# Attention, routed experts and soft experts on one core: a written order of finer steps on every engine up to the experts, and gates made per pair of batches

## The chip, the core and the metric

The kernel runs on one core of a Trainium2 chip. The core has five engines that work side by side, each through its own list of instructions in order: PE (TensorE, matmuls into the accumulation memory PSUM), DVE (VectorE), ACT (ScalarE), POOL (GpSimd) and SP (SyncE, which here only starts DMA transfers). POOL also starts the transfers that gather or scatter rows by an index. An instruction that waits for a semaphore holds up all that stands behind it on its engine. The metric is the device time of one execution in microseconds (us); lower is better.

## The reference

```python
# attention: 8 batches, 8 heads, 576 positions, head size 64
q_s = softmax(q over head dim);  k_s = softmax(k over positions)
kv  = einsum('bhsd,bhse->bhde', k_s, v)
x   = einsum('bhsd,bhde->bhse', q_s, kv)          # laid out as 4608 tokens x 512
# routed experts: 8 experts, 512 -> 1024 -> 512, the best two of each token
logits = x @ w_gate
noisy  = logits + log1p(exp(x @ w_noise)) * noise
top2, top2_w = the two largest of noisy, softmax over the two
out[mask] += top2_w * (relu(x[mask] @ w1[e]) @ w2[e])    # for each expert e
# soft experts on out: 32 slots, softmax over tokens in, softmax over slots out
```

## The kernel before

The 8 batches are worked on as four pairs, numbered 0 to 3; a pair has nine tiles of 128 tokens (TP = 9), 36 tiles in all. The text string FIRST lists the work up to the experts as short steps, and MIX lists the rest of pair 3, which is spread over the first expert blocks, a few steps after each part of a block.

For one pair i the steps are: load k, v and q (`lk`, `lv`, `lq`); the maximum of k over positions, by a DVE maximum over tiles and then PE transposes (`km`); subtract it (`ks`) and take the exponential on ACT (`ke`); the q maximum on DVE (`qm`), its subtraction on POOL (`qs`, L255) and exponential on ACT (`qe`); the product of k and v on PE (`kv`, L277 and L278, four column groups c for each of the two batches b), whose DVE scaling into the tile KB starts with L282; KB transposed and multiplied by the gate weights (`kt`, `kw`); for each of nine tiles j the q transpose on PE (`qt`, L265) and the output product (`ou`, L308), scaled out of PSUM either by DVE (L327, L328) or, with an `a` behind the step, by eight ACT instructions (L324). The scaled tile goes to the table xtab in DRAM. Then `he` adds the eight heads' logits, and `ga` starts a gate: it makes noisy logits, picks the best two experts and counts places. A gate is a generator; each `bg` lets the oldest one go on to its next yield. Before, a pair has two gates, one of six tiles and one of three (GT = 6). Inside a gate, L436 and L437 build a one-hot matrix of rows (`ob`), L445 one of columns (`oa`), and L455 multiplies them on PE.

After the gates of pairs 0 and 1 (18 tiles) `pf` (plan_first) plans the first ten expert blocks: POOL copies eight stretches of a table into the index tile pl_ia (L614), and two gathers (L709) fetch the token rows pl_x of the first block. SP can load that block's weights once pl_eba is known. A block needs its weights split into a high and a low part (L763: R1h on ACT, R1l on DVE, and so on for R2, R0) and its rows transposed on PE (L781) and split (xh on ACT, xl on DVE, L783); then the first expert product runs (L796). MIX runs beside the first nine blocks; the other blocks follow, and a last stage does the soft experts.

What sets the order: FIRST and MIX give only the order in which the program text issues steps. The framework's scheduler then orders each engine's list itself, by its own estimates of durations, so that an instruction can stand well ahead of or behind its place in FIRST.

Of the kernel before, what the change touches and what calls it, by code (L numbers as in the profile page):

```python
# [21 lines left out]
P = 128  # L22
# [14 lines left out]
GT = 6  # L37
# [9 lines left out]
lk0 se lv0 lq0.0 lq0.1 lq0.2 lk1 lq1.0 lq1.1 lq1.2 km0.0 ks0.0 km0.1 qm0.0 qs0.0 qe0.0 qm0.1 qs0.1m qm0.2 ke0.0 ks0.1v ke0.1 qm1.0 km1.0 qs1.0 bg bg kv0.0 kv0.0 kv0.1 kt0.0 qe0.1 qs0.2 ks1.0 kv0.1 kt0.1 qt0.0 qe0.2 kw0.0 lv1 qm1.1 qt0.1 bg km1.1 qt0.2 bg ks1.1 ou0.0 qm1.2 ke1.1 bg bg bg ou0.1 qt0.3 qs1.2 qs1.1 lk2 qt0.4 bg qt0.5 bg ou0.2 kw0.1 ou0.3 bg ke1.0 qt0.6 ou0.4 qt0.7 bg qt0.8 ou0.5a bg qe1.1 he0.1 lq2.0 bg he0.0v qe1.2 lq2.1 ou0.6 lq2.2 ou0.7a qe1.0 bg ou0.8a he0.2 bg bg bg bg bg km2.0 bg bg kv1.0 ga0.0 kv1.0 ga0.1 kt1.0 kv1.1 qt1.0 qt1.1 kw1.0 qm2.0 bg qm2.1 ks2.0 kv1.1 bg ou1.0 km2.1 lv2 kt1.1 qt1.2 ks2.1 bg qm2.2 lq3.0 ou1.1 qs2.0 bg lk3 qt1.3 qs2.2 bg qt1.4 ke2.1 qs2.1 qt1.5 bg kw1.1 ou1.2 bg ou1.3 ou1.4 ze qt1.6 qe2.1 qt1.7 ke2.0 bg he1.0v ou1.5a qt1.8 bg bg bg bg lq3.1 lq3.2 ou1.6a ou1.7 he1.1v ze bg qe2.0 bg ou1.8 bg he1.2 qe2.2 kv2.0 bg ga1.0 ga1.1 pf km3.0 bg bg kv2.0 kt2.0 qm3.0 ks3.0 bg bg qt2.0 kv2.1 kv2.1 km3.1 bg kw2.0 kt2.1 qm3.1 qt2.1 ze lv3 bg qt2.2 ks3.1 qm3.2 qs3.2 ou2.0 qt2.3 ou2.1 qs3.0 ze qs3.1 bg qt2.4 bg bg ou2.2a ke3.1 bg ou2.3 qt2.5 kw2.1 ou2.4a ou2.5a qt2.6 bg bg qt2.7 qt2.8 ou2.6a he2.0 bg bg bg he2.1 qe3.1 ke3.0 ou2.7 bg ou2.8a he2.2 bg bg bg bg bg kv3.0 kv3.0 kv3.1 kt3.0 qe3.2 kw3.0 kv3.1 qe3.0 kt3.1 kw3.1  # L47
# [3 lines left out]
ga2.0 ga2.1 qt3.0 bg bg bg bg bg ou3.0a qt3.1 bg bg bg qt3.2 bg ou3.1a bg qt3.3 ou3.2 bg qt3.4 bg he3.0 ou3.3 bg qt3.5 bg ou3.4 bg bg bg bg ze ze qt3.6 bg ze bg ou3.5a bg bg qt3.7 bg bg ze he3.1 ou3.6a bg ou3.7 qt3.8 ou3.8 bg bg bg bg bg bg bg he3.2 bg bg bg ga3.0 bg ga3.1 bg bg bg bg pl bg bg bg bg bg bg bg bg bg bg bg bg bg bg bg  # L51
# [60 lines left out]
def attention(k):  # L112
# [3 lines left out]
    with ExitStack() as ctx:  # L116
# [72 lines left out]
        def setup():  # L189
# [10 lines left out]
            nc.vector.memset(cnt, 0.0)  # L200
            nc.vector.memset(tab, 0.0)


        def k_max(i, b):
            kt = kts[i]
            m2 = e2.tile([P, 2, D], F32, name="m2")
# [1165 lines left out]
```

## Time and profile before

| | before |
|---|---|
| median of 3 runs | 1235.06 us (1233.3 to 1235.41) |
| profiled execution: its time / the span of its instructions | 1234.64 us / 1232.9 us |
| busy share of the span | PE 93%, DVE 65%, ACT 47%, POOL 27% |
| first expert product (L796) starts | 193.83 us after the span's start |
| PE busy before it / in the rest of the span | 146.89 us of 193.8 / 1001.29 us of 1039.1 |

A timeline row gives start, duration, engine, line, operation, output tile <- input tiles, shape and the number of instructions merged; in brackets stands the idle time of that engine just before, and who ended it. A window row gives for a stretch the busy time of each engine (with its instructions), then the clock granted to PE (1.00 is 2.4 GHz, 0.50 is 1.2 GHz), the mean busy share of the DMA engines and GB/s. PE works on nearly without a break from the first expert product on; ahead of it, it does not.

### The profile page before, as it was taken

To read this page: it belongs to the slowest core of one execution; us is meant where nothing else is said; L and a number is where in the kernel's file an instruction comes from. 1 tells how busy PE (TensorE), PEld (TensorE's weight loads), DVE (VectorE), ACT (ScalarE), POOL (GpSimd) and SP (SyncE) were. 2 spreads that over 40 slices of the span, in tenths; PEclk is the share of its full clock that TensorE was granted. 3 is DMA by queue.
4 is the path that set the end of the run, shared out by engine and by line. 5 is a ranking of instruction groups with operands and counts; after the bars stand their busy time and mean duration, and the time that the engine had idled before them with its cause. 6 is when DMAs were issued, how large, how long until landed. Compare 5 with 4: busy or idle time off the path is not lost. (4 is left out here: it accounts for less than half of the span.)

```text
span 1232.9 us, 21326 instructions
## 1 busy us (share of the span) xinstructions
PE 1148.2 (93%) x7808; PEld 997.7 (81%) x7808; DVE 802.4 (65%) x1493; ACT 580.7 (47%) x879; POOL 326.9 (27%) x376
## 2 busy tenths in 40 slices
PE   6776989999999999999999999999999999969994
PEld 5665878998888998889978998998998998956542
DVE  7889777678876665555556666666666666646653
ACT  3554666464444444434434454544444454424324
POOL 3353251343242322112222322322321321310000
PEclk9788899999999999999999999999999999988997
DMA  9847471796446475556668564563846353237797
GB/s 342 289 143 274 155 263 40 198 290 186 113 106 180 111 215 148 144 163 169 170 176 264 139 199 104 148 193 85 220 108 171 47 151 78 45 69 287 260 356 307
DMA packets 116107, 219.10 MB, mean 178 GB/s; under 512 B 13968, under 2 KB 54032, under 8 KB 111888
## 3 DMA queue, kind: packets, MB, share of 16 engines
q1 hardware_dynamic: 98944, 177.11, 41.8%
q0 software_dynamic: 17040, 40.44, 17.2%
q8 instruction: 67, 1.10, 0.4%
q14 instruction: 56, 0.46, 0.1%
HBM read 243.31 MB, written 49.70 MB: 238 GB/s over the span
## 5 line engine op out<-in xcount | busy, mean ns | idle before, releaser
L763 DVE TENSOR_TENSOR R1l<-ringS,R1h 128x1024 fp32r<-128x1024 f32 x96 | 117.8, 1227 | 102.7 <-ACT R1h L763 100.2
L763 DVE TENSOR_TENSOR R0l<-ringS,R0h 128x1024 fp32r<-128x1024 f32 x95 | 116.4, 1225 | 104.1 <-ACT R0h L763 103.5
L763 ACT ACTIVATE R1h<-ringS 128x1024 fp32r<-128x1024 f32 x96 | 101.7, 1060 | 141.0 <-PE py L826 85.0
L763 ACT ACTIVATE R0h<-ringS 128x1024 fp32r<-128x1024 f32 x95 | 100.8, 1061 | 138.4 <-PE py L826 75.3
L763 DVE TENSOR_TENSOR R2l<-ringS,R2h 128x1024 fp32r<-128x1024 f32 x91 | 111.4, 1225 | 81.2 <-ACT R2h L763 78.7
L763 ACT ACTIVATE R2h<-ringS 128x1024 fp32r<-128x1024 f32 x91 | 96.5, 1060 | 136.2 <-PE py L826 72.6
L796 PE MATMUL ph<-xh,R0h 128*128 128x256 f32 x400 | 113.3, 283 | 2.5 <-ACT R2h L763 2.4
L796 PE MATMUL ph<-xl,R0h 128*128 128x256 f32 x400 | 113.4, 283 | 0.0
L796 PE MATMUL ph<-xh,R0l 128*128 128x256 f32 x400 | 112.9, 282 | 0.0
L800 DVE SCALAR_TENSOR_TENSOR hl<-ph,hh 128x512 fp32r<-128x512 f32 x140 | 95.7, 684 | 24.0 <-ACT hh L799 24.0
L709 POOL DMA_INDIRECT xg<-xtab,pl_idx x40 | 49.2, 1229 | 216.7 <-DVE sc L786 198.1
L796 PE MATMUL ph<-xh,R2h 128*128 128x256 f32 x360 | 102.2, 284 | 1.9 <-DVE hl L800 1.9
L796 PE MATMUL ph<-xl,R2h 128*128 128x256 f32 x360 | 102.0, 283 | 0.5 <-DVE xl L783 0.5
L796 PE MATMUL ph<-xh,R2l 128*128 128x256 f32 x360 | 101.8, 283 | 0.0
L796 PE MATMUL ph<-xh,R1h 128*128 128x256 f32 x360 | 100.7, 280 | 0.2 <-DVE hl L800 0.2
L796 PE MATMUL ph<-xl,R1h 128*128 128x256 f32 x360 | 100.3, 279 | 0.0
L796 PE MATMUL ph<-xh,R1l 128*128 128x256 f32 x360 | 100.3, 279 | 0.0
L832 POOL DMA_INDIRECT x<-y,pl_idx x40 | 63.5, 1588 | 129.0 <-DVE y L831 118.9
L799 ACT ACTIVATE hh<-ph 128x512 fp32r<-128x512 f32 x140 | 81.6, 583 | 32.5 <-PE ph L796 32.5
L826 PE MATMUL py<-R1l,hh 128*128 128x512 f32 x200 | 79.7, 399 | 0.0
L796 PEld LDWEIGHTS ph<-xh,R0h 128*128 128x128 f32 x400 | 76.2, 191 | 3.8 <-ACT R2h L763 2.8
L826 PE MATMUL py<-R1h,hl 128*128 128x512 f32 x200 | 78.8, 395 | 0.0
(439 smaller groups left out, 3064.6 us busy)
## 6 DMA issues: line engine op xcount, KB each, us to landing
ringS<-in_moe_w_dram SPq DMA_DIRECT2D x292, 512.0 KB
ringA<-in_moe_w_dram SPq DMA_DIRECT2D x12, 1024.0 KB
ringA<-in_moe_w_dram SPq DMA_DIRECT2D x22, 512.0 KB
xtab<-xr SPq DMA_DIRECT2D x36, 256.0 KB
kt<-in_k_dram SPq DMA_DIRECT2D x8, 1024.0 KB
v<-in_v_dram SPq DMA_DIRECT2D x8, 1024.0 KB
x<-z SPq DMA_DIRECT2D x5, 1280.0 KB
ringS<-x SPq DMA_DIRECT2D x5, 1024.0 KB
```

The costliest lines, as they stand in the source:

```text
L709: k.nc.gpsimd.indirect_dma_start(out=x, out_offset=None, in_=k.xtab[:n], in_offset=bass.IndirectOffsetOnAxis(ap=idx, axis=0))
L763: turn[1:] = [nc.scalar.activation(r[0], f, AF.Copy), nc.vector.tensor_sub(r[1], f, r[0].bitcast(F32))]
L796: nc.tensor.matmul(ph[:, g, :], w[i][:, c, g * P:(g + 1) * P], x[:, c, :], start=n == 0, stop=n == 11)
L799: nc.scalar.activation(hh[:, fs, :], ph, AF.Relu)
L800: nc.vector.scalar_tensor_tensor(hl[:, fs, :], ph, 0.0, hh[:, fs, :].bitcast(F32), op0=ALU.max, op1=ALU.subtract)
L826: nc.tensor.matmul(py[s], a[h], w[i][:, f, :], start=u == 4 and f == n == 0, stop=u == 7 and f == 1 and n == 2)
L832: d = nc.gpsimd.indirect_dma_start(out=k.x2[:NTOK // 2] if b < NPA else k.x2, out_offset=bass.IndirectOffsetOnAxis(ap=at(b, s), axis=0), i ...
```

## The change

There are four parts.

1. All of FIRST now stands under `tc.manual_schedule` for PE, DVE, ACT, POOL and SP: each engine takes its instructions in the order in which FIRST issues them, and the scheduler only places later work among them. FIRST is rewritten: 439 steps in place of 243.
2. The steps are finer. What one step issued on two or three engines is now one step per engine: k maximum, its transposes, its reduction (`km`, `kn`, `ko`, `kp`), one subtraction and one exponential per part of k (`ks`, `ke` with a third number), q transpose and its copy (`qt`, `qu`), KB scaling, transposes and copies (`kb`, `kt`, `ku`, `kw`, `kx`), and output product, sums, scaling, logits and store (`ou`, then `os oa ol st` or `ov st`). MIX is rewritten too: 135 steps in place of 85.
3. A pair has one gate of nine tiles (GN allots room for 18; each `ga` asks for 9), with a yield between any two engines' turns. The sum of the heads' logits goes to a tile of its own (`ls`). The product of `ge` with the triangle moves from POOL to DVE and both are float16. `ob` is built per three tiles in two buffers.
4. In FIRST, 13 of 27 tiles are scaled by ACT (10 before), the q subtraction of three of twelve groups is on DVE (`qs2.0v`, `qs3.1v`, `qs3.2v`; before, two thirds of one), the head sums of two groups are on DVE (three before). v of pair 0 is loaded after q of pair 0 and k of pair 1 (before: right after k of pair 0). The gate of pair 2 starts in FIRST's last part but is carried on in MIX.

```diff
-GT = 6
+GN, GT = 2 * TP, TP
-lk0 se lv0 lq0.0 lq0.1 lq0.2 lk1 lq1.0 lq1.1 lq1.2 km0.0 ks0.0 km0.1 qm0.0 qs0.0 qe0.0 ...
+lk0 lq0.0 lq0.2 se lq0.1 lk1 lv0 lq1.2 lq1.1 lq1.0 lv1 kf0 km0.0 kg0 kn0.0 qm0.0 km0.1 qs0.0 ...
...
+        def km_tr(i, b):
+            pk = psk["km", i, b] = k.pt([P, 4, P])
...
+        def k_sub(i, b, x):
+            ms = psk["ms", i, b].rearrange("p c d -> p (c d)")
+            kp = k_part(i, b, x)
+            nc.vector.tensor_sub(kp, kp, ms[b * 64:b * 64 + 64] if x == 2 else bcast(ms, 1, 2))
...
         def q_tr(i, j):
-            pq = k.pt([P, 4, P])
+            pq = psk["q", i, j] = k.pt([P, 4, P])
...
+        def q_copy(i, j):
             qTs[i, j] = ap.tile([P, 4, P], F32, name="qT", bufs=4)
-            nc.scalar.copy(qTs[i, j], pq)
+            nc.scalar.copy(qTs[i, j], psk.pop(("q", i, j)))
...
+            eng.tensor_add(lss[i // 2][:, j:j + T1 - T0], lr[:, :, 0], lr[:, :, 1])
-        def gate(T0, T1):
-            n_t = T1 - T0
+        def gate(i, n):
+            T0, n_t = i * TP, n * TP
+            T1 = T0 + n_t
...
-            ge = full("ge", [P, GT, E, E])
+            ge = full("ge", [P, GN, E, E], F16)
+            yield
             nc.vector.tensor_tensor(ge, bcast(n, 2, E), bcast(n, 3, E), op=ALU.is_ge)
-            yield 1
-            nc.gpsimd.tensor_tensor(ge, ge, bcast(k.tril, 1, n_t), op=ALU.mult)
+            nc.vector.tensor_tensor(ge, ge, bcast(k.tril, 1, n_t), op=ALU.mult)
...
+            for h in range(0, n_t, GT):
+                pa = pr.tile([P, E, T1], F32, name="pk")
+                for m0 in range(0, GT, CW // 2):
+                    ms, ml = slice(h + m0, h + m0 + CW // 2), slice(m0, m0 + CW // 2)
+                    ob = sp.tile([P, CW // 2, P, 2], F16, name="ob", bufs=2)
...
-        for st in FIRST.split():
-            step(st)
-        back(99)
+        with tc.manual_schedule(engines={e.engine for e in (nc.tensor, nc.vector, nc.scalar, nc.gpsimd, nc.sync)}):
+            for st in FIRST.split():
+                step(st)
+            back(99)
```

How the lists move, at three places. First PE at the program's start, before (pv is the k-v product, pt a transpose, km the k maximum, mT its reduced form):

```order
L215 MATMUL pt<-ident,kt 128x128 x4
L219 MATMUL pt<-ident,km 128x128 x4
L229 MATMUL pt<-ident,mT 128x128 x4
L219 MATMUL pt<-ident,km 128x128 x4
L277 MATMUL pv<-v_159,kt 128x129 x4
L229 MATMUL pt<-ident,mT 128x128 x4
L278 MATMUL pv<-v_159,kt 128x129
```

and now:

```order
L223 MATMUL pt<-ident,kt 128x128 x4
L240 MATMUL pt<-ident,km 128x128 x8
L251 MATMUL pt<-ident,mT 128x128 x4
L285 MATMUL pt<-ident,q_143 128x128 x12
L251 MATMUL pt<-ident,mT 128x128 x4
L223 MATMUL pt<-ident,kt 128x128 x4
L285 MATMUL pt<-ident,q_143 128x128 x4
L240 MATMUL pt<-ident,km 128x128 x4
L298 MATMUL pv<-v_171,kt 128x129 x4
L299 MATMUL pv<-v_171,kt 128x129
```

The k-v product of pair 0 has moved behind four q transposes and the first transposes of pair 1. Next DVE where the first gate meets the k-v product of pair 1, before (rk is the first DVE instruction behind a k-v product; c, s, dl, rw, ln belong to gates):

```order
L354 TENSOR_SCALAR w<-u 128x24
L400 TENSOR_REDUCE c_815<-s_805 128x8
L360 SCALAR_TENSOR_TENSOR dl<-w,u 128x24
L362 RECIPROCAL rw<-w 128x24
L405 TENSOR_REDUCE s<-n 128x6
L282 TENSOR_SCALAR rk<-pv 128x4
L406 TENSOR_SCALAR s<-s 128x6
L283 RECIPROCAL rk<-rk 128x4
L407 RECIPROCAL s<-s 128x6
L286 TENSOR_TENSOR KB_129<-pv,rk 64x4x64 x2
```

and now:

```order
L402 SCALAR_TENSOR_TENSOR g_701<-ls 128x72
L275 TENSOR_TENSOR q_531<-q_531,qm 128x1536
L307 TENSOR_SCALAR rk<-pv 128x4
L308 RECIPROCAL rk<-rk 128x4
L311 TENSOR_TENSOR KB_131<-pv,rk 64x4x64 x2
L408 TENSOR_SCALAR g_706<-g_703 128x72
L307 TENSOR_SCALAR rk<-pv 128x4
L308 RECIPROCAL rk<-rk 128x4
L311 TENSOR_TENSOR KB_132<-pv,rk 64x4x64 x2
L259 TENSOR_TENSOR kt<-kt,pt 128x1024
L415 SCALAR_TENSOR_TENSOR g_755<-g_706,g_703 128x72
L417 RECIPROCAL g_759<-g_706 128x72
```

The gate's instructions (now 72 columns) stand between whole pieces of pair work, and at this point the gate has only begun. Last, DVE where the first expert block begins, before (R1l, R2l are weight halves, xl the low part of the rows, ob and oa the one-hot matrices of pair 2's gate):

```order
L445 TENSOR_TENSOR oa<-cols,af 128x3x384 x2
L745 MEMSET gn 128x3
L436 TENSOR_TENSOR ob<-cols,bf 128x768 x2
L400 TENSOR_REDUCE c_3466<-s_3459 128x8
L405 TENSOR_REDUCE s<-n 128x3
L763 TENSOR_TENSOR R1l<-ringS,R1h 128x1024
L437 TENSOR_TENSOR ob<-ob,tok_112 128x768
L763 TENSOR_TENSOR R2l<-ringS,R2h 128x1024
L437 TENSOR_TENSOR ob<-ob,tok_112 128x768
L406 TENSOR_SCALAR s<-s 128x3
L763 TENSOR_TENSOR R0l<-ringS,R0h 128x1024
L783 TENSOR_TENSOR xl<-ph_1845,xh 128x4x128
```

and now:

```order
L653 TENSOR_TENSOR pl_done<-pl_done,pl_tf 128x8
L268 TENSOR_REDUCE qm<-qt 128x24
L697 SCALAR_TENSOR_TENSOR pl_at<-pl_done,pl_so 128x8
L774 MEMSET gn 128x3
L275 TENSOR_TENSOR qt<-qt,qm 128x1536
L268 TENSOR_REDUCE qm<-qt 128x24
L812 TENSOR_TENSOR xl<-ph_1747,xh 128x4x128
L815 SCALAR_TENSOR_TENSOR sc,gn<-pl_x_1671,pl_eoa 128x8
L422 SCALAR_TENSOR_TENSOR ln<-ls,ln 128x72
L792 TENSOR_TENSOR R1l<-ringS,R1h 128x1024
L812 TENSOR_TENSOR xl<-ph_1756,xh 128x4x128
```

Pair 2's one-hot matrices are gone from this place, xl stands ahead of the weight halves, and maxima and subtractions of pair 3's q stand in their place.

## Rows read from the trace of the kernel before

**Rows 1.** The page: busy time of each engine, share of the span.

```profile
PE 1148.2 (93%) x7808; PEld 997.7 (81%) x7808; DVE 802.4 (65%) x1493; ACT 580.7 (47%) x879; POOL 326.9 (27%) x376
```

**Rows 2.** Windows: stretch, busy us of each engine, granted clock, DMA share, GB/s.

```profile
0.00:28.00 28.00, 17.23 (x65) 14.01 (x66) 21.47 (x35) 8.81 (x9) 10.12 (x31) 1.00 0.96 335
...
42.00:51.00 9.00, 8.57 (x36) 7.56 (x37) 8.23 (x9) 6.58 (x9) 8.02 (x3) 0.50 1.05 376
...
90.00:130.00 40.00, 28.17 (x197) 24.53 (x197) 35.54 (x99) 20.79 (x43) 12.51 (x12) 0.79 0.69 246
...
168.70:193.80 25.10, 22.07 (x157) 19.11 (x155) 19.19 (x66) 14.36 (x30) 13.97 (x31) 0.93 0.72 237
...
0.00:193.80 193.80, 146.89 (x954) 126.50 (x954) 161.49 (x421) 104.44 (x209) 77.34 (x138) 0.89 0.69 237
...
200.00:300.00 100.00, 100.00 (x674) 90.28 (x673) 73.59 (x153) 54.17 (x90) 28.63 (x40) 1.00 0.68 204
```

**Rows 3.** Timeline of PE: k-v products, first expert product; start us, us, what.

```profile
14.94 2.31 PE L277 MATMUL pv<-v,kt 128*128 128x129 f32 x8 [1.60 <-ACT kt L242]
...
28.91 1.16 PE L277 MATMUL pv<-v,kt 128*128 128x129 f32 x8
...
78.20 2.09 PE L277 MATMUL pv<-v,kt 128*128 128x129 f32 x8 [2.01 <-ACT xr L324]
...
130.86 1.16 PE L277 MATMUL pv<-v,kt 128*128 128x129 f32 x8
...
168.74 1.16 PE L277 MATMUL pv<-v,kt 128*128 128x129 f32 x8
...
193.83 0.36 PE L796 MATMUL ph<-xh,R1h 128*128 128x256 f32 x1
```

**Rows 4.** Timeline of DVE and POOL at the first gate.

```profile
68.27 2.76 POOL L255 TENSOR_TENSOR q<-q,qm 128x1536 f32<-128x1536 f32 x1
...
68.35 2.75 DVE L350 SCALAR_TENSOR_TENSOR na<-lgr 128x48 f32<-128x48 f32 x1 [0.38 <-POOL lgr L336]
```

**Rows 5.** Timeline of DVE: two small gate instructions in a row.

```profile
161.79 0.17 DVE L415 TENSOR_REDUCE pp<-pos 128x3 f32<-128x24 f32 x1
...
161.88 0.17 DVE L418 TENSOR_REDUCE ps<-pos 128x3 f32<-128x24 f32 x1
```

**Rows 6.** Groups of DVE by form to 193.8 us: count, busy us, ns.

```profile
L327 DVE TENSOR_TENSOR xr<-pv,rqa 128x512 f32<-128x512 f32 x17 | 11.6, 682 | 0.1
...
L328 DVE TENSOR_TENSOR lgr<-pv,rqa 128x128 f32<-128x128 f32 x17 | 4.7, 277 | 0.0
...
L257 DVE TENSOR_TENSOR q<-q,qm 128x1024 f32<-128x1024 f32 x1 | 1.2, 1214 | 0.0
```

**Rows 7.** Waits of DVE up to 193.8 us: waiter, releaser, total, times, longest.

```profile
DVE rk L282 <- PE pv L278: 13.0, 6, 3.4
```

**Rows 8.** Timeline of all engines, from the plan to the first expert product.

```profile
170.62 0.22 POOL L614 CAST pl_ia<-pl_m 128x36 f32 x1 [0.28 <-DVE ln L367]
...
177.64 0.25 POOL L614 CAST pl_ia<-pl_m 128x36 f32 x1 [0.15 <-POOL ln L365]
...
180.49 0.96 POOL L709 DMA_INDIRECT pl_x<-xtab,pl_ia  x1 [0.30 <-issue]
...
186.43 1.92 PE L781 MATMUL ph<-ident,pl_x 128*128 128x128 f32 x8
...
187.94 1.21 DVE L763 TENSOR_TENSOR R1l<-ringS,R1h 128x1024 fp32r<-128x1024 f32 x1
...
192.45 0.69 DVE L783 TENSOR_TENSOR xl<-ph,xh 128x512 fp32r<-128x512 f32 x1
```

**Rows 9.** Timeline of PE: q transpose, output product, one-hot product of later pairs.

```profile
152.90 0.60 PE L265 MATMUL pt<-ident,q 128*128 128x128 f32 x4
...
189.41 1.37 PE L308 MATMUL pv<-KB,qT 128*128 128x162 f32 x8 [1.06 <-ACT qT L267]
...
191.05 1.19 PE L455 MATMUL pk<-oa,ob 128*128 128x192 f16 x12
```

More of the change, by code (lines that the diff above doesn't have):

```diff
@@ L201, in setup, with rest_tr, rest_max @@
             nc.vector.memset(tab, 0.0)
+        def rest_tr(i):
+            pk = psk["m8", i] = k.pt([P, 4, P])
+            for c in range(4):
+                nc.tensor.transpose(pk[:, c, :], kts[i][:, 8, c * P:(c + 1) * P], k.ident)
+        def rest_max(i):
+            m8s[i] = sp.tile([P, 4, 2], F32, name="m8", bufs=2)
+            nc.vector.tensor_reduce(m8s[i], psk.pop(("m8", i)).rearrange("p c (b s) -> p c b s", b=2), axis=AX.X, op=ALU.max)
         def k_max(i, b):
@@ L386, in gate @@
[L386 removed]
+            r2 = full("g2")
             nc.vector.tensor_reduce(r2, ge.rearrange("p t e f -> p t f e"), axis=AX.X, op=ALU.add)
[L389 removed]
             nc.vector.tensor_sub(r1, r1, r2)
@@ L425, in gate @@
-            af = full("af", [P, GT, 2], F16)
-            nc.vector.tensor_copy(af, ai)
-            bf = full("bf", [P, GT, 2], F16)
-            nc.vector.scalar_tensor_tensor(bf, af, -float(P), pp, op0=ALU.mult, op1=ALU.add)
-            yield 1
-            ob = sp.tile([P, GT, P, 2], F16, name="ob")
-            parts = [slice(m, m + CW // 2) for m in range(0, n_t, CW // 2)]
-            over = lambda x, ms, n: bcast(x[:, ms], 2, n)
-            for ms in parts:
-                n_p = ms.stop - ms.start
-                nc.vector.tensor_tensor(ob[:, ms], bcast(k.cols[:, :P], 1, n_p), over(bf, ms, P), op=ALU.is_equal)
-                nc.vector.tensor_tensor(ob[:, ms], ob[:, ms], over(k.tok1, ms, P), op=ALU.mult)
-                yield 1
@@ L459, in gate @@
-            if T0 == 0:
-                nc.vector.tensor_copy(tabs, pa)
-            else:
-                tt = sp.tile([P, E * TE], F32, name="tt")[:, :n_c].rearrange("p (e c) -> p e c", e=E)
-                nc.vector.tensor_scalar(tt, pa, 0.0, float(T0 * P), op0=ALU.is_gt, op1=ALU.mult)
-                nc.vector.tensor_add(tabs, tabs, pa)
-                nc.vector.tensor_add(tabs, tabs, tt)
-        bg, fine = [], [False]
+            pi = full("pi", [P, GN, 2], I32)
+            nc.vector.tensor_copy(pi, pp)
@@ L471, in back @@
                 try:
-                    if next(bg[0]) is None or fine[0]:
-                        n -= 1
+                    next(bg[0])
+                    n -= 1
                 except StopIteration:
@@ L540, in attention @@
             pbs[0] = pb
-        fine[0] = True
         yield
```

281 lines of the change are left out of this document (145 added, 136 removed).

## The prediction, made before the change was run

> **What bounds the kernel now.** I read the page first: PE is busy for 93% of the span [rows 1]. The windows say where the other 7% lie. From 200 to 300 us PE is busy for 100.00 us of 100, at the full granted clock; up to 193.8 us it is busy for 146.89 us of 193.8, at a mean clock of 0.89, and no other engine is full either: DVE, the busiest, has 161.49 us [rows 2]. So the kernel has two parts. From the first expert product at 193.83 us on [rows 3] only PE's work counts. Ahead of it is a stage of 194 us that no engine fills, and there the order of the work decides. The change rewrites that order, so its effect is how much earlier the first expert product starts, less whatever PE work it leaves for afterwards.
>
> Within the stage PE's timeline is the best ruler, because every pair has one k-v product that everything else of the pair hangs on. Pair 1's starts at 78.20 us, pair 2's at 130.86, pair 3's at 168.74 [rows 3]. That makes a first cycle of 52.7 us, a second of 37.9, and a tail of 25.1 us from pair 3's k-v product to the first expert product. The first two hold the same kind of work: a k-v product, nine outputs, the gates of a pair. The first one is long for two reasons that the rows show. From 90 to 130 us PE has the mean clock 0.79, so it spends about 40% of that time at 1.2 GHz, and is busy only 28.17 of 40 us, while DVE is busy 35.54 [rows 2]: PE starves behind DVE, its clock falls, and its work then takes longer (eight k-v matmuls 2.31 us at the lower clock at 14.94 us, 1.16 us at the higher one at 28.91) [rows 3]. And DVE itself is held: at the first gate an instruction of 48 columns takes 2.75 us, ending with the POOL subtraction that started just ahead of it and takes 2.76 us [rows 4].
>
> **The change part by part.** DVE's work up to its first weight half: the order has 410 instructions there before and 314 now, 96 fewer. Two gates of nine tiles replace four of six and three, and most of pair 2's gates have moved behind the start of the experts. A small gate instruction takes the engine 0.09 us from start to start [rows 5]; a small one of the output takes 0.277 us [rows 6]. So the saving is between 96 x 0.09 = 9 us and 96 x 0.277 = 27 us. I take 20, nearer the upper row, since one-hot and comparison instructions of hundreds of columns are among those gone. In this count are three tiles fewer to scale on DVE (3 x (0.682 + 0.277) = 2.9 us) and, against it, two q subtractions more at 1.5 x 1.214 = 1.8 us each, less the 1.2 us of the one before [rows 6]. DVE so has about 161.5 - 20 = 141 us to do. With the same 32.3 us of idle time (193.8 - 161.5) the stage would end at 174 us. ACT gets three scaled tiles more; with 104.44 us of 193.8 it covers them [rows 2].
>
> PE's ruler gives the same by another way, and I take the sum from it.
>
> Pair 1's k-v product. v of pair 0 is loaded later: k, q, k and v, 2.36 MB each (nine tiles of 128 x 512 floats), have to come first, 9.4 MB at the 335 GB/s of the first 28 us [rows 2], so that the first k-v product starts near 28 us in place of 14.94. It is eight column groups of about 1.5 us, or twice that at the lower clock, and I expect it to end near 46 us. DVE will stand at its rk for some 10 us there (all such waits together are 13.0 us now [rows 7]). What is gained: by then the maxima of both pairs' k and q are done, work that now stands between the first outputs. Also, nine outputs follow in an order made for them. I take pair 1's k-v product at 75 us, 3 us earlier; the bounds are 7 earlier and 3 later.
>
> First cycle: its lower bound is what the second cycle takes, 37.9 us, its upper one is the present 52.7. I take 39.5, nearer the second cycle, because the causes go: fewer instructions on DVE, ge off POOL, and only three POOL subtractions of q left to run beside gates. Gain 13.2 us.
>
> Second cycle: it is near PE's own pace already; 0, within 2 us either way.
>
> Tail: its chain is the plan, eight POOL copies (170.62 to 177.9 us, with other POOL work between them), two gathers, the second started at 180.49 us, the transposes of the rows at 186.43, and then 7.4 us in which DVE does weight halves and one-hot matrices before it gets to xl at 192.45 [rows 8]. Now the copies stand together on POOL, and xl is ahead of the weight halves, with a q subtraction and maximum of 1.8 us each nearby: I take 3 us off. Against this, the gate of pair 1 ends only as pair 3's k-v product begins, and the plan waits for it: 1 us back. Gain 2; bounds are 5 gained and 3 lost.
>
> Together 3 + 13.2 + 0 + 2 = 18.2 us: the first expert product at 175.6 us.
>
> What PE no longer does before that: four q transposes (4 x 0.60), an output product (1.37), pair 2's one-hot product (1.19) [rows 9], and its place counts (half the one-hot's, as an estimate, 0.5): 5.4 us that have moved into the part in which PE is full, and cost all of it. DVE's share there rises by pair 2's gate and the last q subtractions, some 10 us, beside 73.59 of 100 us [rows 2]: hidden; it would cost up to 3 us if a weight half came late. In total the gates' matmuls do not change (28 a pair, 29 before).
>
> Sum against the profiled execution's own 1234.64 us: 1234.64 - 18.2 + 5.4 = 1221.8. The median of the runs shown, 1235.06, is 0.4 above it, so I say 1222.
>
> A rule can be weighed at one place. The 48-column instruction ends with POOL's subtraction [rows 4]. The Trainium skill, SBUF — State Buffer, section Who interferes with whom, says that a DVE instruction with two SBUF inputs and a GpSimd instruction that reads SBUF exclude each other for the whole instruction. That speaks against a fixed order, in which all of DVE stands behind one such meeting. By that rule, three POOL subtractions beside gates could cost 3 x 2.7 = 8 us, and 1222 would become 1230; without it nothing. The row agrees with the rule, but a meeting needs both at the same moment, and before there were more of both.
>
> **The rivals.** First, a larger gain: the order keeps PE fed and warm, both cycles come down to 36 us and the tail to 20. Then the start moves by 3 + 16.7 + 1.9 + 5.1 = 26.7 us, and the time is 1234.6 - 26.7 + 5.4 = 1213. For it: fewer waits inside each step, and the fine steps allow it. Against: the second cycle of today, 37.9 us, is the best that the trace shows.
>
> Second, nothing to tell: DVE is relieved but PE's pace and clock stay, the first cycle comes down only to 48 us, the rest stays. Then 4.7 us are gained and 5.4 given back: 1235. For it: in the first cycle PE was at the lower clock for much of the time, and a DVE wait of 10 us near 40 us would let the clock fall once more. Against: DVE was busy when PE starved.
>
> Third, slower: head-of-line blocking. In a written order an instruction that comes late holds up all behind it, where the scheduler's order had other work between. The place is pair 0's k-v product, which waits for v behind 7 MB of other loads, with rk and KB of both batches in DVE's list ahead of the next k work. If it runs at the lower clock throughout, and the delay is passed on, pair 1's starts 8 us later, the first cycle takes 50 us and the second 42: + 8 - 2.7 + 4.1 + 5.4 = 15 us, 1249. It decides from the point at which the first expert product starts after 193.8 - 5.4 = 188.4 us. For it: DVE's waits for k-v products are its longest. Against: before, DVE waited there as well, and its instruction count is a quarter less.
>
> That the order is not obeyed is excluded by the lists.
>
> **How the numbers follow.** Forecast 0.52, larger gain 0.25, nothing to tell 0.09, slower 0.14. A measurement of this kernel tells some 0.2% from no change, 2.5 us. Forecast and larger gain are faster, of the second rival a third: 0.80. Same 0.07; slower 0.13. The likeliest case alone, with the bounds of its terms half used, goes from 1215 to 1230. The range for 8 in 10 goes from 1209 (somewhat beyond the larger gain) to 1237 (the second rival and the start of the third).
>
> **What would show it.** Right: the first expert product between 171 and 181 us; pair 1's k-v product near 75 us and 38 to 41 us between the next ones; DVE busy near 141 us before it; PE's granted clock from 90 to 130 us above 0.9; after the start PE full as before, with the rest of the span 5 us longer. Wrong: a first k-v product that ends after 50 us; a first cycle near 50; waits of DVE or PE for one late instruction of 5 us and more in the middle of the stage; or a part after the start that is longer by much more than 5 us, which would mean that PE waits for DVE or ACT in the first blocks.

## The result, and the profile after

The changed kernel takes 1248.13 us (median of 4 runs, 1246.99 to 1249.64) against 1234.18 for the kernel before in the same session: a ratio of 1.0115, with a 95% interval of 1.0095 to 1.0136. It is slower by 14 us; 13 us faster was predicted (1222 after 1235.06). The profiled execution has 1249.64 us, its span 1247.85. The page's first part after, to be laid beside [rows 1]:

```profile
PE 1147.4 (92%) x7804; PEld 997.7 (80%) x7804; DVE 793.5 (64%) x1379; ACT 572.5 (46%) x886; POOL 309.6 (25%) x343
```

No engine has more to do than before: PE 1147.4 us against 1148.2, DVE 9 us less. The span grew by 15 us in which PE stands idle.

Windows of after: two stretches of [rows 2], then the two cycles (from one k-v product of PE to the next), the tail (from pair 3's k-v product to the first expert product), and the rest:

```profile
0.00:193.57 193.57, 137.62 (x909) 119.63 (x910) 143.79 (x316) 90.77 (x212) 62.84 (x112) 0.92 0.65 222
90.00:130.00 40.00, 28.00 (x181) 25.77 (x181) 30.61 (x67) 25.32 (x76) 16.22 (x31) 0.83 0.96 334
74.95:127.36 52.41, 39.48 (x261) 35.19 (x259) 37.19 (x82) 28.10 (x72) 17.00 (x34) 0.87 0.78 271
127.36:168.36 41.00, 33.00 (x256) 29.29 (x252) 32.51 (x87) 22.12 (x66) 6.14 (x16) 0.96 0.17 59
168.36:193.57 25.21, 17.30 (x113) 14.49 (x114) 20.49 (x56) 5.69 (x11) 11.24 (x20) 0.82 0.40 119
...
193.57:1247.85 1054.28, 1009.81 (x6895) 878.03 (x6895) 649.70 (x1064) 481.70 (x675) 246.78 (x232) 0.98 0.57 167
```

The same two cycles, tail and rest of the kernel before, by the starts in [rows 3]:

```profile
78.20:130.86 52.66, 40.83 (x270) 35.25 (x270) 44.47 (x124) 30.60 (x61) 21.06 (x30) 0.80 0.58 203
130.86:168.74 37.88, 33.52 (x264) 29.43 (x262) 32.16 (x125) 25.11 (x64) 11.94 (x33) 1.00 0.44 156
168.74:193.83 25.09, 22.06 (x158) 19.14 (x156) 19.18 (x68) 14.32 (x30) 13.97 (x31) 0.93 0.72 236
193.83:1232.90 1039.07, 1001.26 (x6857) 871.20 (x6855) 640.92 (x1073) 476.23 (x670) 249.51 (x238) 0.98 0.58 167
```

Pair 1's k-v product starts at 74.95 us, as forecast. The first cycle lasts 52.4 us, as long as before, though DVE has 37.2 us to do in it in place of 44.5. The second is 3.1 us longer, which uses up the 3.2 us by which pair 1's product came earlier, and the tail is the same, so the first expert product starts at 193.57 us, where it started before. The rest is 15.2 us longer: PE is busy 8.6 us more in it and idle 6.7 us more.

What PE waits for in the first cycle of after (waiter and releaser; us in total, times, longest):

```profile
PE pv L335 <- ACT xr L362: 6.2, 3, 4.3
PE pv L335 <- DVE lgr L365: 2.3, 1, 2.3
PE pt L325 <- ACT kbT L320: 2.2, 1, 2.2
PE pk L501 <- DVE oa L498: 1.6, 1, 1.6
PE pt L316 <- ACT kbT L320: 0.7, 1, 0.7
```

These five are the whole of its 12.9 us of idle time (52.41 - 39.48): output products that wait for a PSUM tile until ACT (L362) or DVE has scaled it, KB's copies on ACT, and a one-hot matrix. Of the idle time 9.1 us end on ACT. In the first cycle of the kernel before most of it ended on DVE, 9.2 of 11.8 us (52.66 - 40.83):

```profile
PE pk L395 <- DVE tab L460: 3.4, 1, 3.4
PE pk L455 <- DVE ob L437: 2.2, 1, 2.2
...
PE pt L229 <- DVE mT L222: 1.9, 1, 1.9
PE pv L308 <- DVE lgr L328: 1.7, 2, 1.2
```

The tail and the first expert block of after, all engines:

```profile
185.98 0.16 DVE L617 TENSOR_SCALAR pl_eba<-pl_eb 1x10 int32<-1x10 f32 x1
...
186.61 1.75 DVE L268 TENSOR_REDUCE qm<-qt 128x24 f32<-128x1536 f32 x1
...
187.02 7.39 SPq L784 DMA_DIRECT2D ringS<-in_moe_w_dram  x9
...
188.39 1.76 DVE L275 TENSOR_TENSOR qt<-qt,qm 128x1536 f32<-128x1536 f32 x1
...
190.07 1.75 DVE L268 TENSOR_REDUCE qm<-qt 128x24 f32<-128x1536 f32 x1
191.84 0.69 DVE L812 TENSOR_TENSOR xl<-ph,xh 128x512 fp32r<-128x512 f32 x1
191.97 1.06 ACT L792 ACTIVATE R1h<-ringS 128x1024 fp32r<-128x1024 f32 x1 [5.18 <-DMA ringS<-in_moe_w_dram]
...
193.57 0.58 PE L825 MATMUL ph<-xh,R1h 128*128 128x256 f32 x1 [6.55 <-ACT xh L811]
```

Before, the block's expert number and its first weight loads stood here:

```profile
168.46 0.15 DVE L588 TENSOR_SCALAR pl_eba<-pl_eb 1x10 int32<-1x10 f32 x1
```

```profile
169.72 1.64 SPq L755 DMA_DIRECT2D ringS<-in_moe_w_dram  x3
```

The number pl_eba comes at 185.98 us in place of 168.46, so the loads of the experts' weights begin 17.3 us later. ACT's R1h then waits for its load (5.18 us), an xh stands behind it in ACT's list, and PE stands for 6.55 us until that xh is made. DVE meanwhile does three q instructions of pair 3 (1.75 us each) ahead of xl.

### The profile page after: what moved, and what is told of

Its sections match the earlier page's. It is cut to its first block, busy times and chain, and to the rows that moved or that the text cites. A ratio compares the mean times of both kernels' runs of the same rounds, so it can differ in the third digit from the quotient of the medians.

```text
span 1247.9 us, 21149 instructions
## 1 busy us (share of the span) xinstructions
PE 1147.4 (92%) x7804; PEld 997.7 (80%) x7804; DVE 793.5 (64%) x1379; ACT 572.5 (46%) x886; POOL 309.6 (25%) x343
## 5 line engine op out<-in xcount | busy, mean ns | idle before, releaser
L738 POOL DMA_INDIRECT xg<-xtab,pl_idx x40 | 49.8, 1245 | 215.8 <-DVE sc L815 197.2
```

The lines of the kernel that those rows point to most:

```text
L738: k.nc.gpsimd.indirect_dma_start(out=x, out_offset=None, in_=k.xtab[:n], in_offset=bass.IndirectOffsetOnAxis(ap=idx, axis=0))
```

## The experiments

Times are medians; ratios are to the kernel before on the same chip, with 95% intervals. In step strings, {+ +} is added and [- -] taken out. "First cycle" and "start" (of the first expert product) are from the profiled run. The intervals of e7, e13, e14 and e15 lie below that of the change (1.0095 to 1.0136) and that of e10 above it; those of e1 to e6, e9, e11 and e12 overlap with it, so these are read from their traces.

One execution of each was traced, and executions differ. Lists that are alike up to pair 1's k-v product reach it between 74.5 and 75.1 us in some traces and between 76.9 and 77.6 in others. The first cycle of the changed kernel, which e1 and e5 leave as it is, took 52.4, 53.5 and 52.4 us (after, e1, e5), with 13.7, 21.8 and 13.7 us at the lower clock. A difference within these is not told.

### Are the named places the cause?

**e1_plan_early**: the plan's third step, which makes the expert numbers, goes ahead of KB of pair 3.

```
kv3.0.1 ov2.0 bg {+bg+} he2.0v kv3.1.0 st2.0 kb3.0 kv3.1.1 qm3.0 kt3.0 ku3.0 kb3.1 kw3.0 [-bg-] qm3.1
```

> One step of FIRST is moved: the part of the plan that makes the expert numbers pl_eba (and starts the two gathers of rows) is issued behind pair 3's second column group, ahead of KB of pair 3, in place of behind it. Nothing else is edited. In the changed kernel pl_eba is made at 185.98 us, the first weights start at 187.02 and the high half R1h of the first weight waits for its data until 191.97; before they started at 169.72. Theory A (the late expert numbers set the end of the stage): pl_eba near 176 us, weights start near 177 and have landed by 184, the first expert product starts at 186 to 189 in place of 193.57, PE loses no 4 us to the lower clock behind it, and the time falls by 5 to 10 us: 1238 to 1243. Rival B (DVE's list sets it anyway: four q maxima and subtractions of 1.75 us and the weight halves stand ahead of xl): the first expert product stays between 191 and 195 and the time within 3 us of the changed kernel's 1248.

1249.75 us, 1.0102 (1.0067 to 1.0137): nothing gained. The tail of e1:

```profile
180.07 5.01 SPq L784 DMA_DIRECT2D ringS<-in_moe_w_dram  x8
```

```profile
192.95 1.75 DVE L268 TENSOR_REDUCE qm<-qt 128x24 f32<-128x1536 f32 x1
...
201.32 0.69 DVE L812 TENSOR_TENSOR xl<-ph,xh 128x512 fp32r<-128x512 f32 x1
```

```profile
202.93 1.11 PE L285 MATMUL pt<-ident,qt 128*128 128x128 f32 x4 [7.96 <-ACT qt L280]
```

The loads start 7 us earlier, but the first expert product starts at 203.70, 10.1 us later. Of these, 3.6 lie ahead of pair 3's k-v product, where nothing was edited, and 6.5 in the tail. There DVE has the q work of pair 3 and three weight halves ahead of xl, and PE has a q transpose of pair 3 ahead of the first expert product, which waits 7.96 us for its exponential on ACT. The rest is 1046.8 us, 7.5 shorter. So the late number was one of two waits in a row, and lifting it moved time from the rest to the tail.

**e2_swap_scale**: tile 2, ready earlier, is scaled ahead of tile 8, whose place in ACT's list was the 4.3 us wait.

```
qt1.4 bg [-os1.8-] os1.2 {+os1.8+} ks2.0.2 kf3 qu1.4 bg [-oa1.8-] {+oa1.2+} qm2.1 ...
```

> In the changed kernel PE makes the outputs of tile 2 and tile 8 of pair 1 in this order, but DVE and ACT have tile 8's sums and scaling ahead of tile 2's in their lists; PE's next output, which needs the accumulator of tile 2, starts at 105.33 us after a wait of 4.27 us for ACT. Here the two change places in DVE's and ACT's lists (sums, scaling, logits, store), and nothing else. Theory A (an instruction that comes late holds up those behind it in the written lists, and these waits add up to the first cycle of 52.4 us): the third output starts 4 to 5 us earlier, the wait of 4.27 is gone, pair 2's k-v product starts 2 to 5 us earlier than 127.36, the time falls by 2 to 5 us. Rival B (DVE's work sets the first cycle, whatever the order of two tiles): the wait only moves on, pair 2's k-v product starts within 1 us of 127.4 and the time is that of the changed kernel, 1248, within 2 us.

1248.81 us, 1.0104 (1.0070 to 1.0138). The wait fell to 2.0 us, but the one-hot wait rose to 2.5, and the first cycle took 53.7 us, with 19.1 us at the lower clock, about what e1 shows of the unedited cycle (53.5 and 21.8). One wait mended gave nothing that can be told; part of it was taken up by the next.

**e3_free_order**: the same steps, but the scheduler orders them again.

```diff
-        with tc.manual_schedule(engines={e.engine for e in (nc.tensor, nc.vector, nc.scalar, nc.gpsimd, nc.sync)}):
+        if True:
```

> The steps of the changed kernel, its gates per pair and its MIX, but without the written order: the framework's scheduler orders all engines, as before the change. Theory A (the written order itself costs: late expert numbers and head-of-line waits): the first expert product starts at 180 to 190 us and the time is 1232 to 1240. Rival B (the new steps and the pair gates are what costs, order or not; the load of pair 0's v behind 7 MB, the moved work): no better than the changed kernel, 1246 to 1256. Rival C (the written order is better than the scheduler's, and the gain is lost elsewhere): first expert product after 196 us, time over 1252.

1250.77 us, 1.0117 (1.0071 to 1.0163). Its first cycle:

```profile
75.49:137.15 61.66, 47.98 (x272) 40.69 (x273) 41.76 (x97) 33.20 (x82) 14.99 (x34) 0.76 0.67 235
```

The first cycle is 9 us longer than in the written order, the start 13 later (206.78), the rest 9.4 shorter (1044.84). So writing the order is not itself the loss against the kernel before: for these steps the scheduler's order is no better.

**e4_qsub_dve**: the two POOL subtractions of pair 2's q that run beside the first gate go to DVE (`qs2.1v`, `qs2.2v`). In after, L472 of the gate takes as long as the POOL instruction beside it:

```profile
113.82 2.76 POOL L275 TENSOR_TENSOR q<-q,qm 128x1536 f32<-128x1536 f32 x1 [1.38 <-DVE qm L268]
...
113.91 2.76 DVE L472 TENSOR_TENSOR g<-g,s 128x72 f32<-128x72 f32 x1
```

> The two q subtractions of pair 2 that POOL does within the first cycle (2.76 us each, at 105.30 and 113.82 us) are done by DVE in place of POOL (1.75 us each). At 113.91 a gate instruction of 72 columns takes 2.76 us beside one of them, 0.29 elsewhere. Theory A (such meetings set the first cycle): the 72-column instruction takes 0.3 us, pair 2's k-v product starts 2 to 4 us earlier than 127.36, the time falls by 2 to 4 us. Rival B (meetings are small change, waits of the lists decide): DVE's work in the cycle grows by 3.5 - 2.5 = 1 us, pair 2's k-v product starts within 1.5 us of 127.4, the time stays within 2 us of 1248.

1248.93 us, 1.0105 (1.0069 to 1.0141). In e4:

```profile
117.94 0.27 DVE L472 TENSOR_TENSOR g<-g,s 128x72 f32<-128x72 f32 x1
```

The instruction falls from 2.76 to 0.27 us, and the first cycle is 54.3 us, no shorter. DVE's meetings with POOL are not what holds the cycle.

**e8_before_gate9**: the kernel before, with gates of nine tiles (`GT = 9`).

> The kernel before, with one change: one gate of nine tiles per pair in place of one of six and one of three (the steps, the load order and the scheduler's order as before). Theory A (the pair gates are no cost of their own; the loss is in the order and the tail): within 4 us of the kernel before, 1232 to 1240, first expert product at 188 to 198 us. Rival B (a gate that has to wait for its ninth tile comes late and in longer strings, and that is what slows the changed kernel in either order): 1242 to 1252.

1233.75 us, 0.9988 (0.9967 to 1.0008). Gates per pair cost nothing by themselves. The loss lies in the steps and their order; the finer steps, the shares of scaling and the later load of v were not run one by one. Up to pair 1's k-v product they cost nothing: it comes at 74.5 to 77.6 us with them and came at 78.20 before.

### Mending the order

**e5_tail**: the plan's step early as in e1; pair 3's q groups 0 and 1 in the second cycle; group 2 on DVE between the halves of KB; gate 2's work behind the first rows.

> Moving the expert numbers alone changed nothing: the weights then started at 180.07 us, but the first expert product at 203.7, behind four q maxima and subtractions of pair 3 (1.75 us each), a gate and three weight halves in DVE's list. Here, beside the earlier expert numbers, pair 3's q work leaves the tail: two of its three q groups have their maximum (DVE) and subtraction (POOL) in the second cycle, where POOL is busy 6.14 of 41 us, the third has both on DVE in the gap ahead of KB's second half; their exponentials stand ahead of KB's copies on ACT; and the gate of pair 2 is queued on DVE behind the first block's rows. Theory A (the tail is as long as what stands on DVE and ACT between pair 3's k-v product and the rows' xl): from the start of pair 3's k-v product to the first expert product 20 to 22 us in place of 25.2, the part behind it 1044 to 1049 us as in the run before, the time 1235 to 1242. Rival B (the work only moves: two maxima of 1.75 us lengthen the second cycle, in which DVE has 32.5 of 41 us): second cycle 43.5 to 46 us, time 1245 to 1250.

1245.96 us, 1.0083 (1.0058 to 1.0107). The rest came down to 1043.59 us, below the 1044.5 that was forecast for the change, but the start moved to 200.73 us, part of it by two transposes and an output now ahead of it, and by a wait of PE of 4.1 us for a KB copy. The second cycle bore the q work without growing (41.0 us).

**e6_first_cycle**: four waits of the first cycle and one meeting of DVE with POOL mended in the strings (tile 2 scaled and stored first, `ku1.1` ahead of `ke2.1.0`, `qs2.2` on DVE, `ov1.1` earlier).

> The changed kernel with the order of the first cycle (74.95 to 127.36 us) mended in all places where a row shows an engine waiting for one late instruction: ACT copies the second kbT ahead of an exponential (PE waits 2.18 us for it), tile 2 is scaled ahead of tile 8 on DVE and ACT (4.27), tile 1's scaling stands ahead of the gate's string on DVE and ahead of tile 5's (1.60 and 2.26), and one q subtraction of 1.75 us goes from POOL to DVE, so that it doesn't stretch a gate instruction to 2.76 us. No work is added or left out. Theory A (waits in the written lists make the first cycle; one of them alone is taken up by the next, all together are not): pair 2's k-v product starts 43 to 47 us after pair 1's in place of 52.4, the first expert product 5 to 9 us earlier, the time 1239 to 1244. Rival B (each engine's own work and the accumulators' turns make it): 50 to 54 us, time 1246 to 1250.

1246.52 us, 1.0089 (1.0064 to 1.0114). Its first cycle, 2.2 us shorter:

```profile
74.80:124.97 50.17, 39.75 (x261) 34.55 (x259) 37.80 (x83) 28.09 (x72) 12.25 (x31) 0.86 0.79 282
```

PE's wait for scaled tiles fell from 6.2 us to 2.7, that for the one-hot matrix rose from 1.6 to 3.1, and the clock is as low as before. Two more runs have this first cycle: 51.2 us in e7 and 50.2 in e9.

**e7_both**: e5 and e6 together.

> The last two edits together: first cycle and tail. By theory A of both the gains add: first expert product at 178 to 185 us, time 1227 to 1236, about the kernel before or better. If the first cycle can't be shortened by order, but the tail can, it is the tail's run again, 1235 to 1242. If neither, 1246 to 1250.

1242.31 us, 1.0056 (1.0035 to 1.0077): the two gains add up roughly. The third q group had made a wait of its own. In the ACT and PE rows of e7, KB's copy kbT stands behind a q exponential, and PE waits for it:

```profile
184.41 1.48 ACT L280 ACTIVATE qt<-qt 128x1536 f32<-128x1536 f32 x1 [16.69 <-DVE qt L275]
```

```profile
186.42 1.91 PE L325 MATMUL pt<-wbd,kbT 128*128 128x32 f32 x8 [4.10 <-ACT kbT L320]
```

**e9_tail_clean**: e7 with that group moved from FIRST to MIX, to come behind the start, and the first block's weights and rows in a written order.

> In the tail of the last runs my own move stood in the way: the third q group's maximum, subtraction and exponential (1.75, 1.76, 1.48 us) were put between the two halves of KB, ACT's exponential held up the copy of kbT and PE waited 4.10 us for it. Here, with the first cycle mended and the expert numbers early as before, that group goes behind the start (its POOL subtraction too), and the first weight half and the rows of the first block (R1h, xh, xl) stand in a written order of their own right behind KB's copies, ahead of the second weight half. Theory A (the tail is what stands in the lists between pair 3's k-v product and xl): 19 to 22 us from pair 3's k-v product to the first expert product (25.2 in the changed kernel), first expert product at 186 to 191 us, the part behind it 1044 to 1049, time 1231 to 1238, level with the kernel before. Rival B (rows or weights aren't there earlier, and xl waits for DMA): 23 to 26 us, time 1240 to 1244.

1244.06 us, 1.0081 (1.0054 to 1.0109): no gain over e7. The wait of 4.1 us is gone, but the second cycle grew to 46.1 us, of which PE spent 10.2 at the lower clock. The group did not land behind the start: the scheduler put its maximum, subtraction and exponential into the second cycle.

### Does DVE set the first cycle, or PE?

**e10_pe_extra**: eight matmuls of 86 columns, read by nobody, behind each output of pair 1 but that of tile 8.

```diff
+                    for _ in range(2 if i == 1 else 0):
+                        nc.tensor.matmul(po[:, c, NW:NW + 86], qT[:, c, :], KB[i % 2][j // 4][:, c, :86], start=True, stop=True)
```

> The changed kernel with work added to PE in the first cycle alone: behind every output of pair 1 but tile 8's, eight more matmuls of 86 columns into columns of the accumulator that nobody reads, some 0.7 us each tile at the full clock, 5.5 us in all. PE is busy 39.48 us of the first cycle's 52.41 at a mean clock of 0.87. Theory A (the first cycle is set by waits between engines and by the lower clock that follows PE's gaps): the extra work fills gaps, the clock from 90 to 127 us rises, the cycle is 50 to 54 us and the time within 3 us of 1248. Rival B (PE's own work and latency sets the cycle): 57 to 59 us, time 1252 to 1255.

1260.94 us, 1.0211 (1.0175 to 1.0246). First cycle:

```profile
77.56:141.97 64.41, 54.51 (x388) 51.09 (x387) 37.20 (x82) 28.20 (x72) 16.02 (x34) 0.87 0.66 225
```

PE has 15.0 us more to do (54.51 - 39.48), nearly three times the 5.5 expected, so neither forecast's numbers apply; the cycle is 12.0 us longer, some four fifths of it. PE's idle time fell only from 12.9 to 9.9 us, and the clock did not rise. The added work stands inside the outputs, so it also delays the scaling that waits for them.

**e11_dve_extra**: the q maxima of pair 2 are taken twice, three times 1.75 us on DVE.

> The changed kernel with work added to DVE in the first cycle alone: each of pair 2's three q maxima is done twice, 3 x 1.75 = 5.2 us more on DVE, which is busy 37.19 us of the first cycle's 52.41. Theory A (DVE has slack there, and relieving it could gain nothing): the cycle grows by less than 2 us, the time stays within 2.5 us of 1248. Rival B (DVE's list is the chain of the first cycle, though it isn't full): the cycle grows by 4 to 5.5 us, the time to 1252 to 1254.

1250.83 us, 1.0138 (1.0100 to 1.0175). First cycle:

```profile
74.50:130.39 55.89, 40.19 (x261) 35.76 (x259) 43.69 (x85) 28.30 (x72) 17.00 (x34) 0.85 0.75 260
```

3.5 us longer for 5.2 us put in: two thirds, or half against e1's 53.5. PE's wait for the one-hot matrix rose from 1.6 to 4.3 us. Neither engine alone sets the cycle: work added to either lengthens it, by less than what was added.

### The clock

Windows of after at the place where the clock first falls in this cycle:

```profile
88.00:92.47 4.47, 1.61 (x13) 1.13 (x11) 4.38 (x8) 3.99 (x5) 1.59 (x5) 1.00 0.98 356
92.47:99.30 6.83, 6.83 (x33) 6.35 (x34) 3.29 (x5) 3.33 (x7) 0.81 (x4) 0.50 1.02 337
```

PE is busy for 1.61 us of 4.47, in short pieces with gaps of 0.68 and 2.18 us between, and then works 6.83 us at 1.2 GHz.

**e12_fill_gap**: 18 transposes of the identity, read by nobody, in these gaps.

```diff
+        def fill(d, n):
+            for x in range(n):
+                nc.tensor.transpose(d[:, x % 4, :P], k.ident, k.ident)
...
+            if (i, b) == (1, 1):
+                fill(pv_tile(), 4)
...
+            if (i, b) == (1, 0):
+                fd[0] = pv_tile()
+                fill(fd[0], 14)
```

> The changed kernel with 18 transposes of the identity that nobody reads, put into PE's list of the first cycle where PE waits: 4 ahead of the second KB transposes (0.68 us of waiting) and 14 ahead of the gate-weight products (2.18), 0.11 us each at the full clock, so that PE has no gap from 75 to 95 us; no reader waits for them. Theory A (the fall of the clock at 92.47 us follows these gaps, and PE at 1.2 GHz is what makes the cycle long): the clock stays at its upper level past 100 us, the time at the lower level in the cycle falls from 13.7 to 7 us or less, the cycle shrinks by 2 to 4 us, to 48 to 50. Rival B (the clock falls all the same, or its fall is hidden by the waits): 52 to 54 us and the same falls; the time within 3 us of 1248.

1244.80 us, 1.0077 (1.0055 to 1.0100): with 18 useless transposes added it is no slower than after, and by the trace faster. The gap and the stretch behind it (first two rows), then the cycle:

```profile
88.00:92.00 4.00, 3.29 (x27) 2.82 (x27) 3.94 (x7) 3.97 (x5) 1.58 (x5) 1.00 0.94 367
...
92.47:99.30 6.83, 4.89 (x45) 4.25 (x44) 5.69 (x12) 5.31 (x17) 1.59 (x7) 1.00 1.02 327
...
74.50:123.62 49.12, 38.35 (x279) 34.21 (x277) 36.72 (x82) 28.14 (x72) 15.84 (x33) 0.93 0.79 282
```

From 92.47 to 99.30 us PE now does 45 instructions in 4.89 us, where after has 33 in 6.83. PE's other waits in the cycle are what they were (6.2, 2.3 and 1.6 us). The time at the lower clock in the cycle falls from 13.7 to 6.8 us, and the cycle by 3.3, about half of that, as a clock of half the speed makes one expect.

The Trainium skill, TensorE: Matmul & The Clock Gate, section A second HAM failure mode: psum-queue depth-cycling, tells of a kernel whose PE idles briefly but often between groups of matmuls, so that its clock swings between the two levels and throughput is lost. The trace agrees (the clock falls behind gaps of 0.68 and 2.18 us), and e12 shows the price of one such fall, some 3 us.

**e13_fill_mended**: e7 with 12 such transposes there.

> The same idea in the version with first cycle and most of the tail mended (1242.3 us, cycle 51.2, 17.1 us of it at the lower clock): 4 transposes of the identity each ahead of the second KB transposes and of the two gate-weight products, whose waits there are 0.68, 0.68 and 0.67 us. Theory A: the fall at 93.88 us doesn't come, the cycle is 46 to 49 us, the time 1237 to 1241. Rival B: the clock falls at 93 to 95 us as before, cycle 50 to 52.5, time 1241 to 1245.

1239.51 us, 1.0030 (1.0005 to 1.0055). 3.4 us of the cycle at the lower clock, in place of e7's 17.1; the cycle is 46.4 us, not 51.2. It repeats: e15 has the same first cycle and takes 46.4 us with 3.4 at the lower clock, while the same order without the transposes took 50.2 to 51.2 us (e6, e7, e9).

**e15_fill_tail**: e13 with pair 3's third q group moved from FIRST to MIX, to come beside the first expert blocks.

> The version of the run before (first cycle mended, its gaps filled; 1239.5 us) with the last q group of pair 3 taken out of the tail: its maximum, subtraction and exponential are done beside the first expert blocks. PE waited 4.11 us for the copy of kbT behind that exponential. Theory A (that wait and the fall of the clock behind it, 10.2 us at the lower level from 177.2 us on, are tail time): first expert product 4 to 7 us earlier than 190.4, time 1232 to 1236, level with the kernel before. Rival B (rows or weights are late behind it): less than 2 us earlier, 1237.5 to 1240.

1235.96 us, 1.0022 (0.9992 to 1.0052): level with the kernel before, and by the ratios not told from e13. Cycles, tail and rest:

```profile
76.85:123.28 46.43, 36.92 (x272) 32.03 (x271) 37.84 (x83) 28.00 (x72) 14.09 (x31) 0.96 0.76 270
123.28:166.01 42.73, 32.97 (x255) 29.29 (x252) 41.08 (x92) 26.63 (x69) 13.07 (x21) 0.96 0.26 91
166.01:190.54 24.53, 20.30 (x130) 17.52 (x130) 14.59 (x57) 6.88 (x12) 7.16 (x15) 0.86 0.67 234
...
190.54:1234.72 1044.18, 1004.04 (x6882) 872.01 (x6880) 646.05 (x1059) 476.89 (x671) 249.55 (x235) 0.98 0.58 166
```

Against after, pair 1's k-v product starts 1.9 us later, with the same list up to it; the first cycle is 6.0 us shorter, the second 1.7 longer, the tail 0.7 shorter and the rest 10.1 shorter: 13.1 us of the span. The start is where e13 has it (190.54 and 190.38), not 4 to 7 us earlier: the tail fell from 28.4 to 24.5 us, but the group landed in the second cycle here too, and PE waits there for a KB that stands behind it in DVE's list:

```profile
132.73 3.40 DVE L268 TENSOR_REDUCE qm<-qt 128x24 f32<-128x1536 f32 x2
```

```profile
140.10 0.63 PE L324 MATMUL pt<-ident,KB 128*128 128x128 f32 x4 [2.21 <-DVE KB L311]
```

**e14_fill_more**: e15 with further fillers at the start, beside KB of pair 0, and behind one output each of pairs 1 and 2.

> The version with mended first cycle, filled gaps and the mended tail of the other run of this call, and fillers in further gaps of PE: 24 transposes of the identity ahead of pair 1's first maximum (a wait of 4.0 us at 25.8 us, behind which the clock is at its lower level for 6.8 us), four each around KB of pair 0 as for pair 1, and twelve matmuls of 86 columns into unread columns behind one output of pair 1 and one of pair 2, ahead of waits of 3.4 and 3.6 us. Theory A (each fall of the clock in the stage follows a gap and costs): the time at the lower level up to 175 us falls from 16.6 to 8 us or less, the first expert product comes 2 to 4 us earlier than in the other run. Rival B (fillers behind outputs hold up the next output as much as they help; the early fall costs nothing, since pair 1's k work waits for DVE and not for PE): within 1.5 us of the other run.

1240.41 us, 1.0051 (1.0029 to 1.0072). The traced execution, 1244.38, is the slowest of its twelve. The fall of the clock near 29 us (e15) was gone, and pair 1's k-v product came at 73.34 us, ahead of all others. But the first cycle took 49.6 us and the second 45.0: PE had 41.2 and 36.5 us to do in them (e15: 36.9 and 33.0). So by this trace the fillers at the start did no harm, and those behind outputs cost their own time and more.

## Why the prediction was wrong

**What held.** The ruler, and pair 1's k-v product at 75 us (74.95; the same list reached it as late as 77.6 in other traces, so the closeness is luck). The way there held too: the first k-v product ran from 30.84 to 44.5 us (28 to 46 forecast), and DVE stood at its rk for 8.0 us (10). DVE's instructions and work ahead of the start: 314 and 141 us forecast, 316 and 143.79 measured. And gates per pair cost nothing (e8).

One reading needs a note. The prediction reads the lower clock off eight k-v matmuls at 14.94 us, where [rows 2] print 1.00. The trace has no record of the clock ahead of 27.9 us (34.4 in after), and 1.00 is printed where there is none. The durations, 2.31 us against 1.16 at 28.91 [rows 3], bear the reading out; the means of 0.89 before and 0.92 after up to the start are then too high.

**The step that failed first** is the first cycle: "I take 39.5, nearer the second cycle, because the causes go". The causes did go, and the cycle stayed at 52.4 us. DVE's work there fell by 7.3 us, and e4 took away what was left of its meeting with POOL without a gain. "PE starves behind DVE" was right of the kernel before, where 9.2 of PE's 11.8 us of idle time end on DVE. The false step was from there to 39.5: it gave the new lists no waits of their own. In after PE is idle for 12.9 us, in other waits: 9.1 of them for scaling and KB copies that ACT has behind other work in its written list. And part of PE's work again runs at the lower clock. Against the second cycle of the kernel before, from which 39.5 was taken, the first cycle of after has 8.6 us more idle (12.9 and 4.4) and 6.0 us more busy time (39.48 and 33.52), with 13.7 us at the lower clock and none there. The sum over DVE failed at the same point: it kept DVE's idle time at 32.3 us, and it is 49.8 (193.57 - 143.79).

Of the 12.9 us of this miss (52.4 - 39.5) the runs give back some: better places in the lists 2.2 (e6); mended lists and fillers together 6.0 (e13, e15). The 6.9 us that remain to 39.5 were not assigned. In e15 the largest wait left in the cycle is that of PE's one-hot product for the matrix on DVE, 3.5 us; no run took it away.

**The same reason, smaller**: the second cycle, forecast unchanged, is 41.0 us in place of 37.9. It has 3.4 us at the lower clock where before had none, and 8.0 us idle instead of 4.4, 4.9 of them for tiles that ACT scales.

**The tail**, forecast 2 us shorter, is 0.1 longer. "The plan waits for it: 1 us back" was mis-sized. Behind the plan stood not only the gathers but the expert numbers and the weight loads, 17.3 us later than before; and the q work of pair 3, counted as a small item ahead of the start, stood ahead of xl on DVE. I had followed POOL's copies and the gathers, and not SP's loads.

**The rest** was forecast 5.4 us longer and is 15.2 longer. The moved work is as counted: 45 PE instructions fewer ahead of the start (954 to 909). But PE is busy for 8.6 us more and not 5.4, since the first block begins at 1.2 GHz: 8.1 us of its first 15, up to 208.52 us, are at that clock, which costs about half of it. The first 15 us of before, after and e15:

```profile
193.83:208.83 15.00, 15.00 (x123) 14.67 (x122) 9.86 (x30) 9.63 (x27) 1.03 (x3) 1.00 0.11 37
```

```profile
193.57:208.52 14.95, 12.07 (x71) 11.57 (x72) 13.30 (x23) 10.86 (x12) 2.70 (x4) 0.73 0.53 188
```

```profile
190.54:205.54 15.00, 14.83 (x114) 13.83 (x113) 10.72 (x24) 11.89 (x30) 3.10 (x9) 1.00 0.15 44
```

And PE idles 6.7 us more, now at waits that end with an instruction of pair 2's gate, which moved there, or with the rows' low part. The expert product reads nothing of the gate; which result that stands near it in DVE's list PE waited for is not shown.

```profile
PE ph L825 <- DVE cnt L457: 2.4, 1, 2.4
PE ph L825 <- DVE g L444: 2.1, 1, 2.1
PE ph L825 <- DVE xl L812: 1.8, 2, 1.0
```

The prediction had put this gate beside 73.59 us of DVE's 100 and called it hidden [rows 2]; an engine that takes its list in order has no such average. (In both kernels the gate starts with MIX's first step, not in FIRST; before, the scheduler had drawn much of it ahead of the start.) With earlier numbers and less q work beside it the rest fell to between 1043.6 and 1046.8 us (e1, e5, e15); how much each of these was worth is not separated, since the start moved too. In e15 the first block runs at the upper clock and nearly without a break (third of the rows of the first 15 us).

The sum of the misses: 12.9 + 3.1 + 2.1 ahead of the start, less 0.2 by which pair 1's product came earlier than forecast, and 15.2 - 5.4 = 9.8 behind it, together 27.7: from 1221.8 to 1249.5, where the profiled execution has 1249.64.

**The rivals.** The slower one, head-of-line blocking, had the time (1249) and nearly the two cycles (50 and 42 us; 52.4 and 41.0 measured), but not its place, and it had 5.4 us of the 15.2 behind the start: DVE did stand 18.7 us at rk, against 13.0 before [rows 7], and pair 1's k-v product came on time, not 8 us late. That the sum came to 1249 is luck. Its mechanism, one late instruction that holds all behind it, is what the waits of the first cycle for ACT show. It was priced at the program's start alone. The rule on DVE and POOL holds in the trace (2.76 us beside 2.76), but weighed nothing that e4 could show.

## What to carry to other kernels

Relieving a busy engine gains at most the waits that end on it, and a new order brings waits of its own: list the waits of the stage that is to shrink, by releaser, before giving it the time of a better stage, and ask which engine the new lists will make late. A step taken out of the written order goes where the scheduler puts it: look where it landed (e9, e15). When an order is written by hand, follow each number that an address needs to the transfer it releases, and look at every engine's list at the places where the bounding engine waits. Where the matmul engine idles in short gaps, look at the granted clock behind them: 18 useless transposes in two gaps shortened the cycle more (3.3 us) than mending four waits did (2.2).

## What was not expected of the hardware

Eighteen unread transposes in gaps of 0.68 and 2.18 us made the start of the experts 3.7 us earlier (193.57 to 189.84) and the time 1244.80 in place of 1248.13 us, though the two ratios' intervals just overlap; twelve of them in the mended order took 2.8 us off by the medians (e7 to e13; these intervals overlap too). The falls of the clock are not the same in each execution of one list: in the first cycle 13.7 us at the lower clock in after and e5, 21.8 in e1. And an unread matmul of 86 columns cost PE about 0.23 us in this stretch, at both clocks mixed, where 0.09 had been expected (e10: 15.0 us of busy time for 64 of them, 5.5 expected).
